# A mixed attention and long-convolution kernel: softmax shift and sum as identity matmuls, fused parameter steps, an input load in eight chained pieces, a new task order

## The chip, the cores and the metric

The kernel runs on one core of one Trainium2 chip, in one launch. The metric is the device time of an execution in microseconds (us), lower is better. Five instruction queues run side by side on the core: TensorE (PE in the profile, its weight loads PEld), VectorE (DVE), ScalarE (ACT), GpSimd (POOL) and SyncE (SP). Each works strictly through its own list of instructions; a semaphore makes an instruction wait for another queue. POOL and SP here mostly issue DMA transfers.

## The reference

`x` and `u` in the kernel are one tensor, `A_x`, 2048 rows of 640 in bf16 (`B_u` is not read). The result is a gated sum of two branches:

```python
# A: sliding-window attention, H=32 heads of 20, window W=8, dilation 2
qkv = x @ wqkv                                    # [2048,640] @ [640,1920]
logits[h,s,w] = (q[h,s] . k[h,s-2w]) * 20**-0.5   # -1e9 where s-2w < 0
a = (softmax_w(logits) weighted sum of v[h,s-2w]) @ wo
# B: state-space convolution, N=192 complex states per channel
dt = exp(log_dt); P = exp(dt*(A_re + 1j*A_im) * l)          # l = 0..2047
K[d,l] = Re sum_n C[d,n] * P[d,n,l] * dt*B[d,n]
y = irfft(rfft(u, 4096) * rfft(K, 4096))[:2048] + u*Dskip
g = sigmoid((x*gate_w).sum(-1))
out = g*a + (1-g)*y
```

## The kernel before

The program has two halves. The first is a set of some 1,200 small tasks. Each names its engine, a duration, what it depends on, the buffers it takes and gives back, and a due time. `Plan.order` (L91) plays these tasks on a model of the queues and always starts the waiting task with the earliest due time; `Plan.emit` (L185) writes the instructions in the order so found. The due times come from the numbers in `PLAN` (L48). So what stands behind what on each queue is fixed before the launch, and a table of numbers sets it. The second half, `fft_conv` (L959), is written out by hand.

The tasks, in the order in which they become possible:

- **Parameters** (`SSMParams.build`, L544). From C, B, A and dt, all [640,192] and held as 128 x 960 in float32, come the phase step (`tau`, `x1`), the log decay (`xa`), the log magnitude (`xl`) and the angle (`at`) of each state. `tt` (L584) is a two-tensor operation on VectorE, `ts` (L588) a tensor with two scalars, `stt` (L591) a fused (tensor op scalar) op tensor, `act` (L594) a ScalarE function. `ratio` (L634) finds min/max of two magnitudes with a VectorE reciprocal (L637); `angle1` to `angle3` (L652 to L669) set the quadrant; `wrap` (L597) takes a phase modulo 65536 by adding and subtracting a large constant. `split` (L613) cuts each result into two or three bf16 pieces (a ScalarE copy `pc`, L607, and a VectorE remainder, L611), and SP stores the twelve pieces to `Sprm` in DRAM.
- **Transposes and projections.** `window` (L224) turns x into `xT` by identity matmuls (L239). `plan_late` (L302) computes q, k and v: 60 tasks of five 128x512 matmuls (L324), each evicted from PSUM by ScalarE or VectorE (L477/L479) and stored by POOL (L339). ScalarE or VectorE is chosen by the planner for every eviction.
- **Attention** (`plan_core`, L343), in eight chunks of 256 rows. POOL loads `qc`, `kc`, `vc` (L364). Five VectorE products `prod` (L373) go through indicator matmuls into the logits bank `lg` in PSUM (L379), one bank for all chunks. `subtract` (L386): a VectorE maximum over the window (L391) and a VectorE subtraction into `lgs` (L393), which frees `lg`. `expo` (L396): exp on ScalarE. `probs` (L398): VectorE sum (L401), reciprocal (L403), multiplication (L405). SP stores the weights and loads them back spread over partitions (`asb`, L408 and L412). Then five VectorE products with v (L429), identity matmuls that sum over the window (L434), the output projection (L451), and the gate (L460/L462).
- **Convolution kernel** (`KGen.plan`, L718), in ten chunks of 16 channels in each of four groups. SP loads `L` from `Sprm` with eight small transfers (L716), into two buffers; TensorE forms the arguments `ar` (L743, L748); ScalarE takes sin (L760) and exp (L762); VectorE multiplies (`pt`, `qq`, L783 to L785); TensorE sums into `kps` (L801). sin and exp lie in different function tables of ScalarE, each change costs an `ACT_TABLE_LOAD`. After chunks 5 and 10 the half is laid out through DRAM (`KExpand`, L819) and back into `kc`.
- **First transform step** (`first`, L1155): `Usb`, which is x in another layout, and the two halves `kc` are multiplied with `F1c` (L1163). `Usb` shares its memory with `xn`, the buffer of projections (`prj`); its load can only start when the last projection is stored. POOL issues it as four transfers of 640 KB (`rows`, L937; tasks at L1174), followed by `omF` (L943).

The second half multiplies spectra (L994 to L1013), transforms back (L1027, L1047), adds the attention branch and stores.

## Time and profile before

| what | value |
|---|---|
| three runs | 395.54, 396.29, 397.03 us (median 396.29) |
| the profiled execution's own time | 394.38 us |
| its span, first to last instruction | 392.6 us |
| mean granted TensorE clock | 0.923 |
| busy: PE / DVE / ACT / POOL | 319.8 / 333.3 / 307.1 / 79.4 us |
| DMA moved | 58.82 MB |

The profile is of one execution, in microseconds from the first instruction. A row of grouped instructions names source line, engine, operation, output<-input and count, then busy time and the mean duration of one, then the idle time of the engine just ahead of them and what ended most of it. The table of stretches gives, for each stretch of the span, the busy time of each engine (and its number of instructions), the granted TensorE clock (1.00 is full), the busy share of the DMA engines and GB/s. In a row of the timeline the two first numbers are start and duration, and a bracket at its end holds the idle time ahead of it. "issue" stands for a wait for which the profile shows no releaser.

### The profile page before, as it was taken

The page shows a single profiled execution, that of the slowest core. Times are in us where ns is not written, and L with a number is a line of the kernel's source. Part 1 is how long each engine was busy: PE and PEld are TensorE (multiplying, and loading weights), DVE is VectorE, ACT ScalarE, POOL GpSimd, SP SyncE. Part 2 cuts the span into 40 slices and gives each one's busy share as a digit, 9 for nine tenths or more (in the row PEclk, how much of TensorE's full clock was granted, in tenths as well). Part 3 has the DMA queues.
Part 4 walks back from the last instruction along what each step waited for, and adds up shares of the span by engine and source line. Part 5 has one row for each costly group of instructions (what it writes and reads, how often), then busy time and mean ns, then how long its engine had stood idle before and what let it go on. Part 6 is the DMA issues. An engine that isn't in the chain of part 4 may idle for free.

```text
span 392.6 us, 11691 instructions
## 1 busy us (share of the span) xinstructions
PE 319.8 (81%) x5026; PEld 189.5 (48%) x5046; DVE 333.3 (85%) x428; ACT 307.1 (78%) x434; POOL 79.4 (20%) x111
## 2 busy tenths in 40 slices
PE   0299899998979879889676889789999889995770
PEld 0266454443534344454324335446777655554770
DVE  5499999888989999998869785999999459999782
ACT  1489876469889999998769677978977599995791
POOL 8932122320310101004520100100110022100044
PEclk9999999999998989899978656959999999999996
DMA  8965569765721343124995640412481069925046
GB/s 275 372 174 162 175 211 270 206 176 198 216 69 46 104 112 117 45 77 156 193 242 169 203 114 16 127 40 77 155 240 46 35 161 243 225 56 215 2 109 161
DMA packets 51463, 58.82 MB, mean 150 GB/s; under 512 B 36180, under 2 KB 43220, under 8 KB 51156
## 3 DMA queue, kind: packets, MB, share of 16 engines
q1 hardware_dynamic: 41492, 28.78, 27.0%
q0 software_dynamic: 8192, 28.69, 25.0%
q8 instruction: 39, 0.64, 0.7%
q10 hardware_dynamic: 1728, 0.61, 0.6%
q14 instruction: 12, 0.10, 0.1%
HBM read 38.29 MB, written 19.77 MB: 148 GB/s over the span
## 4 chain that ended last, share of the span: by engine, by line
PE 45%; DVE 26%; ACT 14%; issue 6%; DMA 5%; POOL 1%; SPq 1%; POOLq 0%; ACTq 0%; DVEq 0%
PE tb L324 8%; PE tb L434 7%; PE tb L451 5%; PE ar L743 5%; PE fp L994 5%; PE kps L801 5%; PE bp L1163 5%; DVE pv L429 3%; DMA xn<-in_A_x_dram 3%; ACT big L762 3%; ACT sp_u L997 3%; DVE bufA L955 3%; PE lg L379 3%; ACT sp_k L997 3%; DVE qq L785 2%
## 5 line engine op out<-in xcount | busy, mean ns | idle before, releaser
L760 ACT ACTIVATE big<-ar 128x608 bf16<-128x608 int16 x96 | 59.8, 676 | 18.0 <-PE ar L743 9.7
L324 PE MATMUL tb<-bufA 128*128 128x512 bf16 x287 | 70.3, 384 | 4.1 <-DVE prj L479 1.1
L762 ACT ACTIVATE big<-ar 128x864 bf16<-128x864 f32 x60 | 49.6, 909 | 1.9 <-PE ar L743 1.4
L373 DVE TENSOR_TENSOR prod<-qc,kc 128x2048 bf16<-128x2048 bf16 x40 | 47.8, 1219 | 2.2 <-PE lg L379 2.2
L324 PEld LDWEIGHTS <-bufA 128*128 128x128 bf16 x300 | 33.5, 119 | 33.0 <-issue 9.1
L429 DVE TENSOR_TENSOR pv<-vc,asb 128x2048 bf16<-128x2048 bf16 x40 | 47.1, 1218 | 2.6 <-PE tb L434 2.6
L743 PE MATMUL ar<-Rarg,L 64*128 64x304 bf16 (+1 forms) x320 | 39.5, 302 | 6.6 <-ACT big L762 2.6
L434 PE MATMUL tb<-pv,ident 128*128 128x512 bf16 (+1 forms) x185 | 39.3, 352 | 0.9 <-issue 0.5
L801 PE MATMUL kps<-qq,pt 128*32 128x22 bf16 (+1 forms) x2560 | 31.1, 176 | 6.4 <-issue 4.5
L801 PEld LDWEIGHTS <-pt 128*32 128x32 bf16 (+1 forms) x2560 | 24.5, 95 | 21.1 <-issue 15.7
L994 PEld LDWEIGHTS <-PHI 128*128 128x128 bf16 x256 | 24.8, 97 | 19.0 <-issue 8.8
L451 PE MATMUL tb<-wo_sb,oT 128*128 128x320 bf16 x160 | 30.8, 332 | 1.2 <-issue 1.1
L748 PE MATMUL ar<-Rarg,L 64*64 64x304 bf16 (+1 forms) x320 | 22.0, 308 | 11.6 <-issue 4.8
L743 PEld LDWEIGHTS <-L 64*128 64x128 bf16 x320 | 13.6, 96 | 29.3 <-issue 26.3
L477 ACT ACTIVATE prj<-tb 128x512 bf16<-128x512 f32 x30 | 17.8, 596 | 10.5 <-PE tb L324 10.3
L434 PEld LDWEIGHTS <-ident 128*128 128x128 bf16 x192 | 18.0, 100 | 15.9 <-issue 3.2
L997 ACT ACTIVATE sp_k<-fp 128x1280 bf16<-128x1280 f32 x16 | 19.1, 1236 | 4.6 <-DVE om L979 3.0
L994 PE MATMUL fp<-big,PHI 128*128 128x320 bf16 x128 | 19.2, 298 | 3.2 <-ACT sp_k L997 3.2
L785 DVE TENSOR_TENSOR qq<-big 128x1408 bf16<-128x1408 bf16 x24 | 21.2, 884 | 0.0
L451 PEld LDWEIGHTS <-oT 128*128 128x128 bf16 x160 | 15.7, 106 | 11.1 <-issue 4.6
L994 PE MATMUL fp<-bufA,PHI 128*128 128x320 bf16 x128 | 19.1, 298 | 2.3 <-ACT sp_u L997 1.5
L997 ACT ACTIVATE sp_u<-fp 128x1280 bf16<-128x1280 f32 x16 | 19.1, 1237 | 1.8 <-PE fp L994 1.8
(188 smaller groups left out, 601.4 us busy)
## 6 DMA issues: line engine op xcount, KB each, us to landing
asb<-aS SPq DMA_DIRECT2D x8, 512.0 KB, 4.1
PSI<-c_psi SPq DMA_DIRECT2D x8, 512.0 KB, 8.0
PHI<-c_phi POOLq DMA_DIRECT2D x8, 384.0 KB, 5.0
Sprm<-pc SPq DMA_DIRECT2D x12, 240.0 KB, 2.3
L<-Sprm SPq DMA_DIRECT2D x80, 36.0 KB, 2.9
kc<-kS POOLq DMA_DIRECT2D x8, 337.5 KB, 4.3
vc<-vS POOLq DMA_DIRECT2D x8, 337.5 KB, 4.8
xn<-in_A_x_dram SPq DMA_DIRECT2D x4, 640.0 KB, 11.7
```

The lines of the kernel that those rows point to most:

```text
L324: nc.tensor.matmul(ppf, self.wq[:, kt, which * D + e:(which + 1) * D:5], self.xT[:, c0 // 1024, kt, c0 % 1024:c0 % 1024 + SC], start=(kt = ...
L373: nc.vector.tensor_tensor(b[e][:], b["qc"][:, e, :].unsqueeze(1).to_broadcast([128, W, C]), win(b["kc"][:, e, :], 0, W, DIL, C), ALU.mult)
L429: nc.vector.tensor_tensor(b["pv", e][:, :, k, :].rearrange("p w (b t) -> p w b t", t=64), for_e, aw, ALU.mult)
L434: nc.tensor.matmul(b["op", e][:, 0:n, :], ident[:], b["pv", e][:, w, 0:n, :], start=(w == 0), stop=(w == W - 1))
L451: nc.tensor.matmul(apf[:, :320], b["oT"][:, e, i * 128:(i + 1) * 128], wo_sb[:, e, hf * 320:(hf + 1) * 320], start=(e == 0), stop=(e == 4))
L743: nc.tensor.matmul(ar[:, g2, a0:a0 + ncol], L[rows, gp, sb, NST * u:NST * u + 128], R[rows, c0:c0 + ncol], start=True, stop=True, tile_pos ...
L760: nc.scalar.activation(dst[:, 2 * gp:2 * gp + 2, sub, :], ar[:].bitcast(I16)[:, :, 0:2 * SW:2], ACT.Sin, scale=SCL)
L762: nc.scalar.activation(dst[:, 2 * gp:2 * gp + 2].rearrange("p g s n -> p g (s n)"), ar[:, :, 0:2 * EW], ACT.Exp)
L785: nc.vector.tensor_tensor(qq[:], trg[:, :, KI:].rearrange("p a (v m) -> p a v m", v=2), exq[:, :, KI:].unsqueeze(2).to_broadcast([128, 32, ...
L801: nc.tensor.matmul(kps[32 * g:32 * g + 32, c2, NM * ql:NM * ql + NM], pt[rows, k, v, :], qq[rows, k, v, :], start=(g not in started), stop ...
L994: nc.tensor.matmul(fp[:, fl, 0:320].rearrange("p (c x) -> p c x", x=32), PHI[:, fl, kind, :], B[:, :, 2 * f1 + ri].rearrange("p c q g -> p ...
L997: nc.scalar.activation(t[:], fp[:, :, 0:320].rearrange("p f (x g) -> p x f g", g=4), ACT.Identity)
```

## The change

Five things change; the second half of the program is the same.

1. **Softmax.** VectorE still takes the maximum. It then writes the negated maximum as two bf16 tiles of 128x64, `hi` and the remainder `lo`. TensorE adds both into the logits bank with two identity matmuls of 512 columns. exp reads the bank itself and writes bf16. TensorE sums over the window with eight identity matmuls of 64 columns, into the first 64 columns of the same bank. VectorE's reciprocal reads them, and the product is made in place. `lgs` is gone, `at` has two buffers, and the bank is given back only after the reciprocal.
2. **Parameters.** The VectorE reciprocal becomes exp(-ln) on ScalarE and one Newton step on VectorE; many pairs of `ts` and `tt` become one `stt`; the constant steps of `wrap` may go to either engine (`lin`).
3. **Input load.** `Usb` comes in eight transfers of 320 KB. Ahead of each but the first, POOL copies two elements of the piece before, and so waits for its landing.
4. **Added constraints.** The `prod`, `pv` and `pq` tasks keep their chunk order, and the arguments of convolution chunk 8 (c = 7) come after the transposition step of the first half.
5. **Order.** New numbers in `PLAN`, an offset for single tasks, and a few earlier or later readiness times.

```diff
-            ql=119.5, vl=-141.7, pw=2.2, el=-59.4, tl=47.4, vw=0.0, gate=375.0, l=[80.6, 3.2, 98.5, 133.8, 84.1, 71.9, 127.7, 125.4, 107.0, 224.4, 76.7, 167.3],
+            txw=191.1, ql=135.4, vl=-242.7, pw=18.0, el=-653.5, tl=53.4, vw=216.1, gate=2445.0,
...
-             "lgs": 2, "at": 1, "asb": 2, "pv": 2, "oT": 1, "ga": 1, "prj": 4, "prjw": 3, "pc": 4}
+             "at": 2, "asb": 2, "pv": 2, "oT": 1, "ga": 1, "prj": 4, "prjw": 3, "pc": 4}
...
-            t.due = round(t.due, 3)
+            t.due = round(t.due + pr.get("off", {}).get(t.idx, 0.0), 3)
...
-                if act.get(w - 1, 0) < 2930 and x > 25 and not pr.get("warm"):
+                if act.get(w - 1, 0) < 2930 and x > 70 and not pr.get("warm"):
...
-                b["lgs"] = wk.tile([128, W, 64], F32, name="lgs")
-                nc.vector.tensor_tensor(b["lgs"][:], lg[:], mx[:].unsqueeze(1).to_broadcast([128, W, 64]), ALU.subtract)
+                b["hi"] = wk.tile([128, 64], BF16, name="hi", bufs=1)
+                b["lo"] = wk.tile([128, 64], BF16, name="lo", bufs=1)
+                nc.vector.tensor_scalar(b["hi"][:], mx[:], -1.0, None, ALU.mult)
+                nc.vector.scalar_tensor_tensor(b["lo"][:], mx[:], -1.0, b["hi"][:], ALU.mult, ALU.subtract)
+
+            def lower(_, b=b):
+                for k in ("hi", "lo"):
+                    nc.tensor.matmul(b["lg"][:], ident[:], b[k][:].unsqueeze(1).to_broadcast([128, W, 64]), start=False, stop=(k == "lo"), skip_group_check=True)
 
             def expo(_, b=b):
-                nc.scalar.activation(b["lgs"][:], b["lgs"][:], ACT.Exp, scale=scale)
+                b["at"] = wk.tile([128, W, 64], BF16, name="at")
+                nc.scalar.activation(b["at"][:], b["lg"][:], ACT.Exp, scale=scale)
+
+            def total(_, b=b):
+                for w in range(W):
+                    nc.tensor.matmul(b["lg"][:, 0, :], ident[:], b["at"][:, w, :], start=(w == 0), stop=(w == W - 1), skip_group_check=True)
 
             def probs(_, b=b):
-                lg = b["lgs"]
-                sm = wk.tile([128, 64], F32, name="sm", bufs=1)
-                nc.vector.tensor_reduce(sm[:], lg[:].rearrange("p w t -> p t w"), AX.X, ALU.add)
                 rs = wk.tile([128, 64], F32, name="rs", bufs=1)
-                nc.vector.reciprocal(rs[:], sm[:])
-                b["at"] = wk.tile([128, W, 64], BF16, name="at", bufs=1)
-                nc.vector.tensor_tensor(b["at"][:], lg[:], rs[:].unsqueeze(1).to_broadcast([128, W, 64]), ALU.mult)
+                nc.vector.reciprocal(rs[:], b["lg"][:, 0, :])
+                nc.vector.tensor_tensor(b["at"][:], b["at"][:], rs[:].unsqueeze(1).to_broadcast([128, W, 64]), ALU.mult)
...
-            ts(tmp, src, float(mul / 65536.0), MAGIC, ALU.mult, ALU.add)
-            ts(tmp, tmp, MAGIC, 65536.0, ALU.subtract, ALU.mult)
+            lin(tmp, src, mul / 65536.0, MAGIC)
+            lin(tmp, tmp, 65536.0, -MAGIC * 65536.0)
...
-            tt("t0", "t0", "ax", "ay", ALU.max)
-            ts("t0", "t0", 1e-30, None, ALU.max, ALU.bypass)
-            op("recip", "D", 6.1, lambda _: V.reciprocal(t0[:], t0[:]), ["t0"], ["t0"])
+            stt("t0", "ax", 1e-30, "ay", ALU.max, ALU.max)
+            op("act_s0", "A", 0.95, lambda _: SCA.activation(t["s0"][:], t["t0"][:], ACT.Ln), ["t0"], ["s0"], table="ln")
+            op("act_s1", "A", 0.95, lambda _: SCA.activation(t["s1"][:], t["s0"][:], ACT.Exp, scale=-1.0), ["s0"], ["s1"], table="exp")
+            tt("s0", "s0", "t0", "s1", ALU.mult)
+            stt("t0", "s0", 2.0, "s1", ALU.subtract, ALU.mult)
...
-            ts("t0", "wr", 0.0, None, ALU.is_lt, ALU.bypass)
-            ts("t1", "at", -2.0, float(np.pi), ALU.mult, ALU.add)
-            tt("t1", "t1", "t1", "t0", ALU.mult)
-            tt("at", "at", "at", "t1", ALU.add)
+            lin("t1", "at", 1.0, float(-np.pi / 2))
+            stt("t1", "wr", 0.0, "t1", ALU.is_lt, ALU.mult)
+            stt("at", "t1", -2.0, "at", ALU.mult, ALU.add)
...
+            g0, h0 = (n - 1) // 2, (n - 1) % 2
+            nc.gpsimd.tensor_copy(P["pace"][32 * g0:32 * g0 + 32, :], P["Usb"][32 * g0:32 * g0 + 32, 32 * h0, 0:2])
+        nc.gpsimd.dma_start(P["Usb"][32 * g:32 * g + 32, 32 * h:32 * h + 32], x.rearrange("(a b) d -> a b d", b=64)[:, 32 * h:32 * h + 32, 160 * g:160 * g + 160])
```

What the new numbers do is seen in the order of the instructions. Rows are those of the built program, without their numbers; equal neighbours are merged (x2), and L is the source line of the version concerned.

**VectorE around the phase step and the reciprocal of the parameters, before** (`t_143` and `t_144` are two scratch tiles, `ax` and `ay` the magnitudes, `aim` the input that comes last):

```order
L586 TENSOR_TENSOR wr<-wr,t_143 128x960
L586 TENSOR_TENSOR wi<-wi,t_144 128x960
L586 TENSOR_TENSOR tau<-aim,dtb 128x960
L589 TENSOR_SCALAR s_154<-tau 128x960
L479 CAST bufA<-ar 128x1024
L589 TENSOR_SCALAR s_154<-s_154 128x960
L592 SCALAR_TENSOR_TENSOR tau<-tau,s_154 128x960
L586 TENSOR_TENSOR t_143<-ax,ay 128x960
L589 TENSOR_SCALAR t_143<-t_143 128x960
L637 RECIPROCAL t_143<-t_143 128x960
L611 TENSOR_TENSOR s_154<-tau,pc 128x960
```

**and now:**

```order
L604 TENSOR_TENSOR wr<-wr,t_144 128x960
L604 TENSOR_TENSOR wi<-wi,t_145 128x960
L654 TENSOR_TENSOR dt_139<-dtb 128x5
L610 SCALAR_TENSOR_TENSOR t_144<-ax,ay 128x960
L604 TENSOR_TENSOR t_145<-ax,ay 128x960
L604 TENSOR_TENSOR tau<-aim,dtb 128x960
L604 TENSOR_TENSOR xl<-xl,xa 128x960
L604 TENSOR_TENSOR xl<-xl,dt_139 128x960
L610 SCALAR_TENSOR_TENSOR tau<-tau,s_155 128x960
L492 CAST bufA<-ar 128x1024
L637 TENSOR_TENSOR s_155<-tau,pc 128x960
```

Maximum and minimum of the magnitudes stand ahead of the step that reads `aim`, the two constant steps of the wrap have left VectorE at this place, and the reciprocal is gone.

**VectorE at the softmax of the second attention chunk, before** (`prj<-tb` evicts a projection, `pv` is a product with v of the chunk ahead):

```order
L391 TENSOR_REDUCE mx<-lg 128x64
L393 TENSOR_TENSOR lgs<-lg,mx 128x512
L479 CAST prj<-tb 128x512 x3
L401 TENSOR_REDUCE sm<-lgs 128x64
L403 RECIPROCAL rs<-sm 128x64
L405 TENSOR_TENSOR at<-lgs,rs 128x512
L479 CAST prj<-tb 128x512
L429 TENSOR_TENSOR pv<-vc,asb 128x8x256 x4
```

**and now:**

```order
L395 TENSOR_REDUCE mx<-lg 128x64
L398 TENSOR_SCALAR hi<-mx 128x64
L399 SCALAR_TENSOR_TENSOR lo<-mx,hi 128x64
L442 TENSOR_TENSOR pv<-vc,asb 128x8x256 x2
L492 CAST prj<-tb 128x512 x2
L415 RECIPROCAL rs<-lg 128x64
L416 TENSOR_TENSOR at<-at,rs 128x512
L377 TENSOR_TENSOR prod<-qc,kc 128x2048 x5
```

Two products with v and two evictions stand between maximum and reciprocal, where three evictions stood; the products of the next chunk come behind the reciprocal.

**POOL around the load of `Usb`, before** (`qS` is the store of a projection, `qc`, `kc`, `vc` are loads for attention, `Kx` the layout of the first convolution half):

```order
L364 DMA vc<-vS 128x5x270
L364 DMA kc<-kS 128x5x270
L339 DMA qS<-prj 640x1x512
L940 DMA Usb<-in_A_x_dram 32x64x160 x4
L943 DMA omF<-omS 32x128 x2
L364 DMA qc<-qS 128x5x256
L364 DMA vc<-vS 128x5x270
L943 DMA omF<-omS 32x128 x2
```

**and now:**

```order
L343 DMA vS<-prj 640x1x512
L343 DMA qS<-prj 640x1x512
L970 DMA Usb<-in_A_x_dram 32x32x160
L969 COPY pace<-Usb 32x2
L970 DMA Usb<-in_A_x_dram 32x32x160
L368 DMA qc<-qS 128x5x256
L368 DMA kc<-kS 128x5x270
L368 DMA vc<-vS 128x5x270 x2
L969 COPY pace<-Usb 32x2
L970 DMA Usb<-in_A_x_dram 32x32x160
L969 COPY pace<-Usb 32x2
L970 DMA Usb<-in_A_x_dram 32x32x160
```

One piece at a time is under way, and the attention loads stand between the pieces; the first piece follows the last two stores of projections directly.

More of the change, by code (lines that the diff above doesn't have):

```diff
@@ L412, in spread @@
                 nc.sync.dma_start(b["asb"][:].rearrange("p b x -> p (b x)"), self.aS[sc % 2].rearrange("h b x -> h (b x)").unsqueeze(1).to_broadcast([32, 4, W * C]))
[L413 to L416 removed]
+            mx = pl.add(f"max{sc}", "D", 0.90, top, deps=[l], due=due(5 * pr["pw"]))
+            ng = pl.add(f"neg{sc}", "P", 0.45, lower, deps=[mx], due=due(5 * pr["pw"]), eq=1024)
+            ex = pl.add(f"exp{sc}", "A", 0.55, expo, deps=[ng], acq=["at"], due=due(5 * pr["pw"] + pr["el"]), table="exp")
+            sm = pl.add(f"sum{sc}", "P", 0.40, total, deps=[ex], due=due(5 * pr["pw"] + pr["el"]), eq=512)
+            at = pl.add(f"at{sc}", "D", 1.17, probs, deps=[sm], rel=[("lg", lgs[0])], due=due(5 * pr["pw"] + pr["el"] + pr["tl"]))
+            st = pl.add(f"ast{sc}", "S", 0.4, store, deps=[at], rel=[("at", ex)], due=due(0.0), dma=0.45)
             asb = pl.add(f"asb{sc}", "S", 0.55, spread, deps=[st], acq=["asb"], due=due(0.0), dma=1.6)
@@ L577, in build @@
         tau, x1, xa, xl_, at, s0, s1 = (f(n) for n in ("tau", "x1", "xa", "xl", "at", "s0", "s1"))
+        bias = {}
+        for c in (MAGIC, -MAGIC * 65536.0, 1e-36, float(-np.pi / 2)):
+            bc = pin.tile([128, 1], F32, name=f"bc{len(bias)}")
+            nc.vector.memset(bc[:], c)
+            bias[c] = bc[:]
         ops = []
@@ L671, in build @@
         for step in [weights, phase, squares, st[0], ratio, size, st[1], st[2], lambda: wrap("x1", "tau", 256.0, "t0"), sl[0], sl[1], angle1, sx[0],
[L672 removed]
+                     sx[1], angle2, sx[2], lambda: tt("xa", "xa", "are", "dtb", ALU.mult, rdy=21.0), sa[0], angle3, sa[1], sp[0], sp[1]]:
             step()
@@ L806, in plan @@
                 due = d0 + dd * (0.55 + 0.16 * u) + pr["dl"][c]
-                p = pl.add(f"pq{c}{u}", "D", 2.04, products, deps=ends[u, 0] + ends[u, 1], acq=["pq"], rel=[("trg", held[u, 0]), ("exq", held[u, 1])], due=due)
+                p = pl.add(f"pq{c}{u}", "D", 2.04, products, deps=ends[u, 0] + ends[u, 1], after=self.pqs[-1:], acq=["pq"], rel=[("trg", held[u, 0]), ("exq", held[u, 1])], due=due)
                 self.pqs.append(p)
```

79 lines of the change are left out of this document (43 added, 36 removed), and 3 rows, old and new, of the table f0.

## The prediction

> **What bounds the kernel now.** I read the span first, then the table of stretches, then the rows in the stretch where all engines fall off together. The stretches are cut where the work changes: from 17 us the input is there, 59 ends most of the parameters, 100 to 265 is convolution kernel and attention together, from 309.6 the second half runs.
>
> ```profile
> span 392.6 us, 11691 instructions
> ...
> 17.00:59.00 42.00, 38.80 (x287) 23.57 (x292) 40.25 (x40) 35.68 (x47) 12.26 (x19) 1.00 0.63 193
> 59.00:100.00 41.00, 39.22 (x228) 17.83 (x232) 36.51 (x46) 28.49 (x43) 11.07 (x14) 1.00 0.71 210
> 100.00:185.00 85.00, 73.45 (x1879) 38.73 (x1883) 81.28 (x111) 77.72 (x117) 9.32 (x11) 0.94 0.34 102
> 185.00:200.00 15.00, 9.99 (x266) 5.04 (x262) 10.12 (x13) 9.04 (x16) 7.39 (x10) 0.84 1.04 192
> 200.00:265.00 65.00, 54.74 (x1109) 27.96 (x1107) 55.35 (x71) 53.53 (x77) 5.58 (x9) 0.70 0.43 127
> 265.00:309.60 44.60, 44.03 (x564) 32.81 (x567) 39.91 (x56) 36.85 (x50) 3.19 (x5) 1.00 0.37 114
> 309.60:392.60 83.00, 58.84 (x709) 43.11 (x707) 61.47 (x88) 61.32 (x85) 14.78 (x24) 0.96 0.59 143
> ```
>
> The columns behind the length are PE, PEld, DVE, ACT and POOL busy, the granted clock, the DMA share and GB/s. VectorE is busy for 40.25 of 42 us while the parameters are made and for 81.28 of 85 us in the middle; TensorE has 39.22 of 41 from 59 to 100 and 44.03 of 44.6 from 265. So VectorE limits two stretches, TensorE two. From 185 to 200 nothing is full but the DMA engines (1.04), and from 200 to 265 the clock is 0.70 and VectorE down to 55.35 of 65. The rows of the hole:
>
> ```profile
> 183.40 4.20 POOL L940 DMA_DIRECT2D Usb<-in_A_x_dram  x4 [4.00 <-PE ar L743]
> 184.47 6.13 SPq L716 DMA_DIRECT2D L<-Sprm  x8
> 198.22 0.46 PE L748 MATMUL ar<-Rarg,L 64*64 64x304 bf16 x1 [4.82 <-issue]
> 198.78 0.68 ACT L760 ACTIVATE big<-ar 128x608 bf16<-128x608 int16 x1 [4.62 <-PE ar L748]
> 199.71 0.69 DVE L391 TENSOR_REDUCE mx<-lg 128x64 f32<-128x512 f32 x1 [4.88 <-PE lg L379]
> ...
> DMA to landing us min/median/max: 2.9/11.0/15.3
> ```
>
> The last line is of the `L` loads from 170 to 202 us. POOL issues the four parts of `Usb` at once; the eight small `L` transfers that SP issues a microsecond later need up to 15.3 us instead of 2.9. The argument matmul of the next chunk reads `L`; it stands for 4.82 us, and ScalarE (4.62) and VectorE (4.88) behind it.
>
> **The change part by part.** The sum is made against the profiled execution's own 394.4 us (span 392.6 and 1.8 around it); the median of the three runs, 396.3, lies 1.9 higher, and the predicted time is for the median.
>
> *Parameters.* Durations:
>
> ```profile
> L637 DVE RECIPROCAL t<-t 128x960 f32<-128x960 f32 x1 | 6.2, 6152 | 0.0
> L589 DVE TENSOR_SCALAR t<-t 128x960 f32<-128x960 f32 x4 | 2.8, 710 | 0.1
> L586 DVE TENSOR_TENSOR t<-t,t 128x960 f32<-128x960 f32 x3 | 3.5, 1152 | 0.0
> L592 DVE SCALAR_TENSOR_TENSOR tau<-tau,s 128x960 f32<-128x960 f32 x1 | 1.2, 1159 | 0.0
> ...
> L607 ACT ACTIVATE pc<-s 128x960 bf16<-128x960 f32 x7 | 7.0, 1000 | 0.5 <-DVE s L611 0.3
> L595 ACT ACT_TABLE_LOAD x2 | 2.6, 1283 | 0.0
> ...
> 15.27 1.16 DVE L586 TENSOR_TENSOR tau<-aim,dtb 128x960 f32<-128x960 bf16 x1 [3.73 <-DMA aim<-in_B_A_im_dram]
> ```
>
> By the order, VectorE loses the reciprocal (6.15), 7 of 13 two-scalar operations (7 x 0.71 = 5.0) and 6 of 26 two-tensor ones (6 x 1.15 = 6.9), and gains 9 fused ones (9 x 1.16 = 10.4): 7.6 us less. ScalarE gains four operations of 1.0 and one table load of 1.28 here (five stand in this part instead of four, 17 instead of 18 in the program): 5.3 us beside VectorE, covered as long as ScalarE keeps up; it has 35.68 of 42 us now, so what it gains must partly be taken from it, and the order does that (below). Maximum and minimum now stand in the 3.73 us in which VectorE waits for `aim`: up to 2 us more. That pays for a new wait in the first softmax, where only one eviction stands between maximum and reciprocal (some 2 us by the chain worked out under the third rival); I count both as nothing.
>
> *Softmax.* Durations, the last row but one being the smallest VectorE operation with two scalars:
>
> ```profile
> L391 DVE TENSOR_REDUCE mx<-lg 128x64 f32<-128x512 f32 x8 | 5.5, 688 | 6.8 <-PE lg L379 6.6
> L393 DVE TENSOR_TENSOR lgs<-lg,mx 128x512 f32<-128x512 f32 x8 | 5.5, 692 | 0.3
> L401 DVE TENSOR_REDUCE sm<-lgs 128x64 f32<-128x512 f32 x8 | 8.3, 1032 | 0.9 <-ACT lgs L396 0.8
> L403 DVE RECIPROCAL rs<-sm 128x64 f32<-128x64 f32 x8 | 4.4, 553 | 0.3
> L405 DVE TENSOR_TENSOR at<-lgs,rs 128x512 bf16<-128x512 f32 x8 | 5.5, 692 | 0.3
> ...
> L266 DVE TENSOR_SCALAR omg<-g_sb 128x16 f32<-128x16 f32 x1 | 0.2, 174 | 0.0
> ...
> L396 ACT ACTIVATE lgs<-lgs 128x512 f32<-128x512 f32 x8 | 5.1, 631 | 0.0
> ```
>
> Subtraction (0.69) and sum (1.03) go in each of eight chunks: 13.8 us. Maximum, reciprocal and product stay, and I leave their prices. `hi` and `lo` are new, 16 operations on 64 columns, between 0.17 (16 columns) and 0.55 (the 64-column reciprocal, which is slow for its size): 2.8 to 8.8 us. I take 0.2 each, near the plain operation, 3.2 us. VectorE saves 10.6, with ends of 5.0 and 11.0. exp stays one instruction of about 0.63.
>
> TensorE's added work is bounded by these rows:
>
> ```profile
> 176.93 1.90 PE L434 MATMUL tb<-pv,ident 128*128 128x512 bf16 x8
> ...
> L255 PE MATMUL ar<-gw_sb,bufA 128*128 128x1 bf16 x80 | 2.1, 163 | 0.0
> L239 PE MATMUL ar<-ident,xn 128*128 128x128 bf16 x80 | 7.7, 256 | 14.2 <-DMA xn<-in_A_x_dram 13.7 <-ACT bufA L477 0.3
> ```
>
> Sixteen matmuls of 512 columns at 1.90/8 = 0.24 are 3.8 us. The 64 of 64 columns lie between 2.1/80 = 0.026 (1 column) and 7.7/80 = 0.096 (128): 1.7 to 6.1 us, taken in the middle at 0.06, 3.8. Together 7.6.
>
> *Evictions.* The new order gives ten evictions from ScalarE to VectorE.
>
> ```profile
> L479 DVE CAST prj<-tb 128x512 bf16<-128x512 f32 x15 | 10.2, 684 | 2.3 <-PE tb L324 2.1
> L479 DVE CAST big<-bp 128x1024 bf16<-128x1024 f32 x3 | 3.7, 1220 | 0.5 <-PE bp L1163 0.5
> L477 ACT ACTIVATE prj<-tb 128x512 bf16<-128x512 f32 x30 | 17.8, 596 | 10.5 <-PE tb L324 10.3
> ```
>
> Four have 512 columns (4 x 0.68), two net have 1024 (2 x 1.22), four are narrower (0.68 at most, taken at 0.45): 6.9 us onto VectorE. ScalarE loses about the same, which pays for its 5.3.
>
> VectorE's net is -7.6 - 10.6 + 6.9 = -11.3 us. Its work from 17 to 265 stands now at 40.25 + 36.51 + 81.28 + 10.12 + 55.35 = 223.5 in 248 us.
>
> *Input load.* The prices and the first reader:
>
> ```profile
> kc<-kS POOLq DMA_DIRECT2D x8, 337.5 KB, 4.3
> ...
> L940 POOL DMA_DIRECT2D Usb<-in_A_x_dram x4 | 4.2, 1058 | 4.0 <-PE ar L743 4.0
> L975 POOL COPY PSI<-sp_u 128x2 bf16<-128x2 bf16 x4 | 3.4, 841 | 2.1 <-ACT sp_u L997 2.1
> ...
> L1163 PEld LDWEIGHTS <-Usb x80: 158/161/163, 274.8 to 309.2; 128*128 128x128 bf16 x80
> ```
>
> With one piece under way, an `L` load meets 320 KB instead of 2.6 MB; a transfer of that size lands in 4.3 us, so the 4.9 us hole (VectorE's 4.88) goes. A piece costs POOL at most an issue of 1.06, a landing of 4.3 and a copy of 0.84, 6.2 us, eight of them 50. Even if the chain starts at 183.4 as now, it ends near 233, ahead of the first reader at 274.8 (some 259 after the gain); by the order it starts earlier, since the last projection stores stand earlier. Behind each waiting copy stand attention loads (`qc`, `kc`, `vc`) and behind the last the store of `Kx`; a load can come up to 6.2 us late. I price that at nothing, because those loads are issued ahead of their products.
>
> The added order constraints and the 83.0 us of the second half cost nothing: same instructions, same order.
>
> **Sum:** -11.3 (VectorE) - 4.9 (hole) = -16.2; 394.4 - 16.2 = 378.2 for an execution like the profiled one, 380 for the median.
>
> What is late next is TensorE. It has 38.80 + 39.22 + 73.45 + 9.99 + 54.74 = 216.2 us of work from 17 to 265, and 223.8 with 7.6 more, in a stretch of 232. That is 96%; the best the trace shows before 265 is 78.0 of 83 us, 94%. The sum therefore needs part of the slow clock of 200 to 265 back. I expect that, because the hole stands right ahead of the fall from 0.94 to 0.70.
>
> [...]
>
> **The rivals.**
>
> *TensorE becomes the bound.* The clock stays at 0.70 where it is 0.70, because between 200 and 265 no wait of TensorE is long:
>
> ```profile
> PE kps L801 <- issue: 2.0, 2, 1.4
> ```
>
> This is the longest there, 1.4 us, so the low clock can have a cause other than the hole, and the change adds two waits of TensorE per chunk (for `lo`, for exp). Then 223.8 us at 94% need 238 us: -10, 384.4, 386 for the median, and 389 with the dearer small matmuls. Against it: the clock was 0.94 to 1.00 until the hole. Chance 0.24. [...]
>
> *The clock comes back fully.* From 200 to 265 VectorE works at the share of 100 to 185 (81.28/85 = 0.956 instead of 55.35/65 = 0.852): 65 x 0.104 = 6.8 us more, -23, 373 for the median. For it: every stretch without the hole ahead of it is at 0.94 or better. Against: it asks for 98% of TensorE unless the faster clock shortens its work. Chance 0.15.
>
> *Slower: the softmax becomes a chain through three in-order queues, on one bank.* Between maximum and product now lie `hi`/`lo`, two matmuls, exp, eight matmuls and the reciprocal. One hand-over costs what VectorE loses at a product:
>
> ```profile
> 70.22 1.23 DVE L373 TENSOR_TENSOR prod<-qc,kc 128x2048 bf16<-128x2048 bf16 x1 [0.31 <-PE lg L379]
> ```
>
> Four of 0.31, with 0.4 + 0.48 + 0.63 + 0.5, are 3.2 us, 4.5 with a table load. If TensorE reaches the sum before exp is done, the arguments and `kps` matmuls behind it wait, and ScalarE and VectorE after them; and no next logits can start while the bank is held. It decides from 16.2/8 = 2 us lost per chunk. At 3 us, 24 in all, the time is 402, 404 for the median. Against it: in all chunks but the first, four to eleven operations stand between `lo` and the reciprocal on VectorE, 3 us and more. Chance 0.10.
>
> That the change does nothing, because the work it takes off VectorE lay under TensorE's time everywhere, would need -4.9 to be lost as well: 0.03.
>
> **How the numbers follow.** The forecast has 0.48, 380. The range runs from 368 (the second rival with the cheaper end of the unknown prices, and a little of the clock for TensorE) to 392 (the first rival with `hi` and `lo` at the dear end); it leaves out the slower case and tails, about 0.15. A measurement of this kernel tells about 0.5% (2 us; the three runs lie 1.5 apart) from no change. Faster: 0.48 + 0.24 + 0.15, less the upper tail of the first rival, 0.85. Slower 0.10, same 0.05.
>
> **What would show it.** Right: VectorE's work from 17 us to the second half down by about 11; the `L` loads landing within 6 us and no idle above 2 us on PE, ACT and DVE at once; a second half of 83 us. The first rival shows as PE above 94% busy with a clock near 0.7; the third as idle time on VectorE ahead of the reciprocal (L415) and on TensorE ahead of its sum (L411) of 2 us per chunk. The parameter term is wrong if VectorE waits for ScalarE before 55 us, the load term if VectorE waits for products of a late `vc` or TensorE for `Usb`.

## The result and the profile after

| | before | after |
|---|---|---|
| median of four runs each | 396.66 us (395.54 to 397.70) | 384.59 us (384.40 to 385.24) |
| profiled execution, its span | 394.38, 392.6 us | 384.76, 383.0 us |
| first matmul of the second half | 311.0 us | 302.0 us |

The ratio is 0.9732, with an interval of 0.9686 to 0.9778: faster, by 12.1 us in the medians and by 8.8 to 12.5 us by the ratio's interval on 396.7 us. The forecast was 380 (368 to 392), a gain of 16. The gain of the profiled executions, 9.6 us, lies in the first half (9.0). Here and below, the ratios leave out executions over 1.5% above the fastest of their kernel (two of them, of 1,493 and 710 us, far above), while medians are of all.

The profile after, first the span and the busy times, then the same stretches as before (PE, PEld, DVE, ACT, POOL busy, clock, DMA share, GB/s; the second half now begins at 302):

```profile
span 383.0 us, 11863 instructions
...
PE 316.9 (83%) x5102; PEld 191.0 (50%) x5126; DVE 323.0 (84%) x437; ACT 304.1 (79%) x427; POOL 89.3 (23%) x122
```

```profile
17.00:59.00 42.00, 35.07 (x266) 21.27 (x271) 38.55 (x40) 37.54 (x47) 12.86 (x20) 0.96 0.72 212
59.00:100.00 41.00, 39.34 (x279) 17.76 (x279) 30.38 (x44) 28.38 (x43) 8.80 (x11) 1.00 0.54 160
100.00:185.00 85.00, 77.40 (x1720) 41.42 (x1731) 79.02 (x105) 74.33 (x113) 16.79 (x23) 1.00 0.52 144
185.00:200.00 15.00, 14.10 (x471) 7.82 (x470) 14.65 (x30) 12.66 (x20) 10.41 (x7) 0.93 0.47 117
200.00:265.00 65.00, 55.77 (x1330) 30.54 (x1331) 59.09 (x84) 55.66 (x78) 7.31 (x13) 0.83 0.42 121
...
300.00:383.00 83.00, 60.52 (x714) 44.96 (x712) 62.23 (x88) 61.74 (x85) 14.71 (x24) 0.93 0.63 143
```

VectorE's work fell by 333.3 - 323.0 = 10.3 us (forecast 11.3); from 17 us to the second half it fell by 12.4, since some of it moved ahead of 17. The stretch from 185 to 200 has lost its hole: TensorE has 14.10 us of work in it instead of 9.99. The clock from 200 to 265 rose from 0.70 to 0.83, not to 1. From 59 to 100 TensorE is as full as before and VectorE now idles 10.6 us: there its saving became waiting.

The prices of the new softmax, by groups (busy, mean ns, idle time ahead):

```profile
L407 ACT ACTIVATE at<-lg 128x512 bf16<-128x512 f32 x8 | 4.8, 605 | 0.0
...
L415 DVE RECIPROCAL rs<-lg 128x64 f32<-128x64 f32 x8 | 4.4, 553 | 2.1 <-PE lg L411 1.9
...
L403 PE MATMUL lg<-hi,ident 128*128 128x512 bf16 x8 | 3.3, 413 | 0.0
...
L411 PE MATMUL lg<-at,ident 128*128 128x64 bf16 x64 | 3.2, 193 | 0.2
...
L398 DVE TENSOR_SCALAR hi<-mx 128x64 bf16<-128x64 f32 x8 | 2.1, 257 | 0.3
...
L399 DVE SCALAR_TENSOR_TENSOR lo<-mx,hi 128x64 bf16<-128x64 f32 x8 | 1.8, 225 | 0.3
```

`hi` and `lo` cost 0.24 each (taken at 0.2), the 64 small matmuls 3.2 us (taken at 3.8). The 413 ns of a matmul on `hi` is its own length; the one on `lo` starts 0.22 to 0.26 us behind it in seven chunks of eight, near the 0.24 taken. Ahead of the reciprocal VectorE waits 2.1 us in all eight chunks together.

The timeline of TensorE just ahead of the hole of before; then that of the kernel after where it stops now; then, after, the time of the `L` loads from issue to landing:

```profile
192.96 0.45 PE L748 MATMUL ar<-Rarg,L 64*64 64x304 bf16 x7
```

```profile
212.62 0.64 PE L826 MATMUL kps<-qq,pt 64*32 64x22 bf16 x63
215.88 0.41 PE L826 MATMUL kps<-qq,pt 64*32 64x22 bf16 x33 [2.61 <-issue]
```

```profile
DMA to landing us min/median/max: 1.7/2.6/5.1
```

Before, the seven matmuls are a whole task of four and three of the next, all of one chunk. The fourth of that next task, which reads the same `L`, came only at 198.22; TensorE had stopped at 193.4 us. The earlier tasks of the chunk (L743, up to 191.6 us) had read every part of this `L`, so no wait for `L` can stand there. The prediction had the wrong cause. After, `L` lands in 5.1 us at most, and TensorE again stops in the middle of a task, for 2.61 us.

What both stops have in common is in the DMA table. Its row of the instruction queue, after:

```profile
q8 instruction: 40, 0.66, 0.7%
```

Forty packets, each of 16,384 bytes in the trace; TensorE's list has 5,126 matmuls and as many weight loads, so a packet would hold some 256 of its instructions, or 128 pairs (an estimate: 2 x 5,126 / 40). The times of these packets, taken from the trace, against the end of each wait of TensorE for "issue" (us):

```
kernel   wait of TensorE   it goes on at   packet lasted        goes on after its end by
before        4.82            198.22       195.32 to 196.77          1.45
before        1.44            230.25       227.84 to 228.93          1.32
before        1.14            111.88       109.20 to 110.27          1.61
after         2.61            215.88       213.61 to 214.57          1.31
after         0.79            137.50       135.01 to 135.90          1.60
```

In thirteen profiles of this case (before, after and the eleven kernels of the table below) TensorE has 67 waits of over 0.4 us for "issue". Every one of them ends 1.20 to 1.61 us after such a packet has ended. Every one also stands at the same place of TensorE's list: counted in weight loads from its start, 92 or 93 past a multiple of 128, whatever the instruction there is. That is the estimated size of a packet, and I read it so: TensorE had run out of instructions, and the packet with the next ones was late. This rests on these times and counts; no run shows the instructions themselves arriving. Below, waits for instructions are waits of this kind. In the first row of the table the packet started only 1.9 us after TensorE had stopped. (A first profile of the kernel before with the pieces, the execution of 1,493 us, is not among the thirteen: it has 20 such waits, of 0.74 to 0.94 us, none of which ends 1.2 to 1.6 us after a packet, and their cause is open.)

### The profile page after: what moved, and what is told of

Its sections match the earlier page's. It is cut to its first block, busy times and chain, and to the rows that moved or that the text cites. A ratio compares the mean times of both kernels' runs of the same rounds, so it can differ in the third digit from the quotient of the medians.

```text
span 383.0 us, 11863 instructions
## 1 busy us (share of the span) xinstructions
PE 316.9 (83%) x5102; PEld 191.0 (50%) x5126; DVE 323.0 (84%) x437; ACT 304.1 (79%) x427; POOL 89.3 (23%) x122
## 4 chain that ended last, share of the span: by engine, by line
PE 51%; ACT 19%; DVE 13%; DMA 9%; issue 5%; SPq 1%; POOL 1%; POOLq 0%; ACTq 0%; DVEq 0%
PE tb L328 13%; PE tb L447 7%; PE ar L768 6%; PE fp L1024 5%; PE tb L464 5%; PE kps L826 4%; PE bp L1195 3%; DMA aim<-in_B_A_im_dram 3%; ACT big L787 3%; ACT sp_u L1027 3%; ACT big L785 3%; PE lg L383 3%; DVE bufA L985 3%; ACT sp_k L1027 3%; PE ar L773 2%
## 5 line engine op out<-in xcount | busy, mean ns | idle before, releaser
L328 PE MATMUL tb<-bufA 128*128 128x512 bf16 x283 | 71.5, 388 | 6.5 <-DVE bufA L492 2.1
L785 ACT ACTIVATE big<-ar 128x608 bf16<-128x608 int16 x96 | 59.6, 677 | 10.2 <-PE ar L768 9.4
L768 PE MATMUL ar<-Rarg,L 64*128 64x304 bf16 (+1 forms) x320 | 37.0, 290 | 5.8 <-ACT big L785 2.4
L826 PE MATMUL kps<-qq,pt 128*32 128x22 bf16 (+1 forms) x2560 | 30.2, 175 | 4.6 <-issue 4.2
L826 PEld LDWEIGHTS <-pt 128*32 128x32 bf16 (+1 forms) x2560 | 23.3, 93 | 17.5 <-issue 12.3
L464 PE MATMUL tb<-wo_sb,oT 128*128 128x320 bf16 x160 | 27.7, 310 | 0.0
L490 ACT ACTIVATE prj<-tb 128x512 bf16<-128x512 f32 x28 | 16.5, 598 | 10.9 <-PE tb L328 9.9
L959 POOL DMA_DIRECT2D PHI<-c_phi x8 | 4.5, 558 | 79.5 <-PE fp L1024 41.7
L773 PE MATMUL ar<-Rarg,L 64*64 64x304 bf16 (+1 forms) x320 | 19.6, 298 | 3.8 <-ACT big L787 1.6
L243 PE MATMUL ar<-ident,xn 128*128 128x128 bf16 x80 | 7.9, 263 | 15.6 <-DMA xn<-in_A_x_dram 14.1
## 6 DMA issues: line engine op xcount, KB each, us to landing
PSI<-c_psi SPq DMA_DIRECT2D x8, 512.0 KB, 10.2
xn<-in_A_x_dram SPq DMA_DIRECT2D x4, 640.0 KB, 12.4
```

The source lines that it names most:

```text
L328: nc.tensor.matmul(ppf, self.wq[:, kt, which * D + e:(which + 1) * D:5], self.xT[:, c0 // 1024, kt, c0 % 1024:c0 % 1024 + SC], start=(kt = ...
L464: nc.tensor.matmul(apf[:, :320], b["oT"][:, e, i * 128:(i + 1) * 128], wo_sb[:, e, hf * 320:(hf + 1) * 320], start=(e == 0), stop=(e == 4))
L768: nc.tensor.matmul(ar[:, g2, a0:a0 + ncol], L[rows, gp, sb, NST * u:NST * u + 128], R[rows, c0:c0 + ncol], start=True, stop=True, tile_pos ...
L773: nc.tensor.matmul(ar[64 * h:64 * h + 64, g2, a0:a0 + ncol], L[rows, h, sb, m0:m0 + 64], R[rows, c0:c0 + ncol], start=True, stop=True, til ...
L785: nc.scalar.activation(dst[:, 2 * gp:2 * gp + 2, sub, :], ar[:].bitcast(I16)[:, :, 0:2 * SW:2], ACT.Sin, scale=SCL)
L826: nc.tensor.matmul(kps[32 * g:32 * g + 32, c2, NM * ql:NM * ql + NM], pt[rows, k, v, :], qq[rows, k, v, :], start=(g not in started), stop ...
```

## The experiments

Theory A is the prediction's: VectorE sets the pace of the first half, what is taken from it is passed on, TensorE's new work lies beside it, and the pieces take the late `L` loads away. Theory B: TensorE has become the bound. On the load the rival is the late instruction packet. All times are of several timed runs beside the kernel before; ratios are to it, and "on the kernel after" is the difference of the ratios times 396.7 us. By both intervals, taken as independent, such a difference is uncertain by 2.2 to 2.7 us, by 3.3 for the four dense matmuls alone and by 3.6 for `Kx` spread.

| kernel | median us | ratio (interval) | on the kernel after |
|---|---|---|---|
| after, old softmax | 395.57 | 0.9986 (0.9948 to 1.0023) | +10.1 |
| after, more matmuls | 395.13 | 0.9990 (0.9958 to 1.0022) | +10.2 |
| after, old reciprocal | 389.46 | 0.9831 (0.9782 to 0.9880) | +3.9 |
| after, `Usb` at once | 396.42 | 1.0034 (1.0000 to 1.0067) | +12.0 |
| before, with pieces | 392.54 | 0.9926 (0.9887 to 0.9965) | (-2.9 on before) |
| after, old softmax and reciprocal | 398.35 | 1.0038 (0.9992 to 1.0084) | +12.1 |
| after, `Kx` spread | 382.48 | 0.9646 (0.9567 to 0.9726) | -3.4 |
| after, four dense matmuls | 387.52 | 0.9829 (0.9759 to 0.9899) | +3.8 |
| `Kx` spread, useless burst | 384.35 | 0.9721 (0.9679 to 0.9762) | -0.4 |
| `Kx` spread, no `lo` | 381.02 | 0.9610 (0.9559 to 0.9661) | -4.8 |
| the last, four dense matmuls | 381.83 | 0.9628 (0.9578 to 0.9678) | -4.1 |

**Old softmax in the new order.**

```diff
-                nc.vector.tensor_scalar(b["hi"][:], mx[:], -1.0, None, ALU.mult)
-                nc.vector.scalar_tensor_tensor(b["lo"][:], ...)
+                nc.vector.tensor_tensor(b["lgs"][:], lg[:], mx[:]..., ALU.subtract)
...
-                nc.tensor.matmul(b["lg"][:], ident[:], b[k][:]..., ...)
...
-                    nc.tensor.matmul(b["lg"][:, 0, :], ident[:], b["at"][:, w, :], ...)
+                nc.vector.tensor_reduce(sm[:], b["lgs"][:]..., AX.X, ALU.add)
```

> The kernel after with the old softmax put back in its place, all tasks in the new order: VectorE subtracts the maximum and sums over the window (8 x (0.69 + 1.03) = 13.8 us) instead of writing hi and lo (2.1 + 1.8 = 3.9 us), TensorE gives up the two shift matmuls and the eight sums of every chunk (3.3 + 3.3 + 3.2 = 9.8 us by their rows, some 7 by throughput). Theory A, VectorE sets the pace of the first half and its work is passed on one for one: +9.9 us on the kernel after. Theory B, TensorE sets the pace since the change: VectorE's 9.9 us hide and TensorE's 7 to 9.8 us come off, so -7 to 0. Between the two (+2 to +7): the engines are so evenly loaded that work moved between them counts in part.

+10.1 us: theory A's number. VectorE's 9.9 us were worth their full time, although the matmuls went away with them. The number is not VectorE's alone: in this profile TensorE waits 8.3 us for instructions up to the second half (waits over 0.4 us; 4.8 after), and 11 windows of slow clock stand there where the kernel after has 8.

**More matmuls.**

```diff
             def total(_, b=b):
+                for _k in range(4):
+                    nc.tensor.matmul(b["lg"][:], ident[:], b["at"][:], start=True, stop=True, skip_group_check=True)
```

> The kernel after with four more identity matmuls of 512 columns ahead of every window sum, whose result the sum overwrites: 32 x 0.24 = 7.7 us more on TensorE, nothing on VectorE or ScalarE. Theory A (VectorE sets the pace): within 1 us of the kernel after. Theory B (TensorE sets the pace): +7 us or more. A third reading is that more activity keeps TensorE's clock up, which would make it faster.

+10.2 us for 7.7 us of work: theory B's side. Added work on TensorE is not free. In the profile TensorE is busy 15.2 us longer (332.1 against 316.9), and two of the extra slow windows come late, from 255 and 371 us. Its waits for instructions sum to 7.9 us instead of 4.8; with the 7.7 that makes 10.8, so a late packet may be what made the work dearer than its price. So neither theory holds alone: from this balance, work added to either engine is paid. Why taking TensorE's work away in the run before gave nothing back stays open; the waits named there are a candidate.

**Old reciprocal.**

```diff
-            stt("t0", "s0", 2.0, "s1", ALU.subtract, ALU.mult)
+            op("stt_t0", "D", 1.1, lambda _: V.reciprocal(t["t0"][:], t["t0"][:]), ["s0", "s1"], ["t0"])
```

with the logarithm, the exponential and the product ahead of it left out.

> The kernel after with the parameter reciprocal back on VectorE in the place of the last Newton operation, everything else in the new order: VectorE gains 6.15 and loses 1.16 + 1.16, +3.8 us; ScalarE loses two operations of 1.0 and a table load of 1.28. Theory A (VectorE sets the pace): +3.8 us on the kernel after. Theory B (the parameters lie under TensorE's work): 0. If ScalarE is what the parameters wait for: -2.

+3.9 us, theory A. In the profile the first maximum of the softmax stands 3.6 us later (74.3 against 70.7): passed on from the start. The close agreement of the total is partly luck, since its uncertainty is 2.7 us and the waits for instructions differ too (8.0 us in this profile, the longest of the six executions, against 4.8).

**`Usb` at once.**

```diff
-            nc.gpsimd.tensor_copy(P["pace"][...], P["Usb"][...])
-        nc.gpsimd.dma_start(P["Usb"][32 * g:32 * g + 32, 32 * h:32 * h + 32], ...)
+        for g in range(4):
+            nc.gpsimd.dma_start(P["Usb"][32 * g:32 * g + 32], ...)
```

> The kernel after with Usb loaded as four transfers of 640 KB at once, at the place of the first piece, without the waiting copies; the order of all engines but POOL stays. The prediction's theory, late L loads: L lands some 10 us late, TensorE's first argument matmul of a convolution chunk waits for a DMA, +4.9 us on the kernel after. Rival, the instruction fetch: TensorE stands 3 to 5 us in the middle of a task, with no releaser in the profile, and goes on 1.3 to 1.6 us after a 16 KB packet of the instruction queue has ended; no wait for L stands ahead of it. If the burst at this place does not fall on a stretch in which TensorE takes short instructions, both give 0, and the attention loads, no longer behind waits for landing, come earlier: -1.

+12.0 us, and neither number: the burst starts at 152.9 us, and what it hits there is a third thing. VectorE, then TensorE, in that run:

```profile
163.39 0.42 DVE L492 CAST oT<-tb 128x256 bf16<-128x256 f32 x1 [0.69 <-PE tb L447]
172.89 1.01 DVE L475 TENSOR_SCALAR ga<-tb,g_sb 128x320 bf16<-128x320 f32 x2 [9.08 <-DMA gaS<-ga]
...
177.41 4.63 DVE L442 TENSOR_TENSOR pv<-vc,asb 128x2048 bf16<-128x2048 bf16 x4 [2.32 <-DMA vc<-vS]
```

```profile
173.50 1.49 PE L464 MATMUL tb<-wo_sb,oT 128*128 128x320 bf16 x5 [7.73 <-DVE ga L475]
```

VectorE waits 9.08 us for the store of the chunk ahead, which was issued at 158.26 and has the buffer `ga`, then 2.32 for `vc`. The loads of `vc` issued from 152 to 172 us landed in 17.5 us, against 4.9 in the kernel after. Here the burst delayed the transfer that was needed next; which one that is depends on the order. Both explanations of the load term were too narrow.

**Pieces alone, in the kernel before.** The rows are those of the kernel after; POOL issues the first piece where the four transfers stood and the others between the attention loads behind.

```diff
-        nc.gpsimd.dma_start(P["Usb"][32 * g:32 * g + 32], ...)
+            nc.gpsimd.tensor_copy(P["pace"][...], P["Usb"][...])
+        nc.gpsimd.dma_start(P["Usb"][32 * g:32 * g + 32, 32 * h:32 * h + 32], ...)
```

> The kernel before, all engines in its own order; only POOL loads Usb in eight chained pieces, the first where the four transfers stood, the others between the attention loads behind. Both theories on the hole (late L loads, late instruction fetch) expect the 4.8 us wait of TensorE at 193 us to go: -4.9 us on the kernel before. If the slow clock from 195 to 263 us came from the hole, it goes too: -10 to -12 in all. If the pieces are worth nothing by themselves, 0, and the gain of the kernel after is that of its other parts.

> A second profile of the kernel before with the pieces alone, 392.54 us in the timed runs, since the first profiled execution was disturbed. Late instruction fetch: no wait of TensorE over 2 us near 193 us, and smaller ones that each end 1.2 to 1.6 us after an instruction packet; the slow windows from 195 on fewer than 13, by two or three only, since a gain of 3 us leaves no room for more. If the 4.8 us wait is still there, the pieces gained elsewhere.

-2.9 us (1.4 to 4.5) where 4.9 were forecast. The second profile, 389.54 us, shows the place on the timeline (L752 is L748 of before), and the `L` loads from 170 to 202 us:

```profile
193.51 0.45 PE L752 MATMUL ar<-Rarg,L 64*64 64x304 bf16 x7
195.83 0.31 PE L752 MATMUL ar<-Rarg,L 64*64 64x304 bf16 x1 [1.88 <-issue]
```

```profile
DMA to landing us min/median/max: 1.8/4.7/5.0
```

The wait is down from 4.82 to 1.88 us, between the same two matmuls, with `L` landing in 5.0 us at most; it ends 1.20 us after a packet of the instruction queue. Of 13 slow clock windows from 195 us to the second half 9 are left, and 14 of 16 from the start.

**Old softmax and old reciprocal together** (both edits above).

> The kernel after with both the old softmax and the old reciprocal, in the new order: what is left of the change are the order, the pieces, the other parameter steps and the constraints. If the two costs add up as measured one by one (+10.0 and +3.9 on the kernel after): 398 to 399, no better than the kernel before. If they hide each other in part: 393 to 396. If VectorE had not been what limits: 385 to 388.

398.35 us, ratio 1.0038: the two costs add up nearly (12.1 against 14.0). So order, pieces, evictions and the other parameter steps together are worth +1.5 us (-0.3 to +3.3) against the kernel before, where the prediction's terms for them make -3.75 - 4.9 + 6.9 = -1.75.

**`Kx` spread.** At 208 us the kernel after sends 1.3 MB of `Kx` at once, from SP and POOL.

```diff
+            if hf == 0:
+                if e == "S":
+                    return
+                for n in (0, 2):
+                    nc.gpsimd.dma_start(Kx[n:n + 2]..., x[:, n:n + 2, 0:8]...)
+                    nc.gpsimd.tensor_copy(x[:, n, 0, 0:2], x[:, n, 0, 0:2])
+                nc.gpsimd.dma_start(Kx[4:8]...[1], x[1::2, 4:8, 1:9]...)
+                nc.gpsimd.tensor_copy(x[:, 4, 8, 0:2], x[:, 4, 8, 0:2])
```

> The kernel after with the three stores of Kx for the first convolution half (1.28 MB at once at 208 us) sent by POOL as four of 320 KB, each behind the landing of the one before, and the four loads of kc behind them, on POOL too. Theory, bursts hold up the instruction fetch: the 2.6 us wait of TensorE at 213 us goes, and with it the idle window that starts the six slow clock windows from 215 to 235 us; -2.6 from the wait alone, up to -10 with the clock. Rival, the slow windows come from the small matmuls there and not from the wait: -1 to -3. Cost: kc lands near 240 us instead of 223, ahead of its first matmul at 246; if it is later than that, TensorE waits for it and the gain is lost.

-3.4 us in the timed runs, not clear of the 3.6 us of uncertainty, and between the numbers of theory and rival (a profiled execution of 377.3 us span against 383.0). Stretches after, then with `Kx` spread, columns as above:

```profile
210.00:220.00 10.00, 6.79 (x231) 3.35 (x231) 7.25 (x10) 6.82 (x10) 1.68 (x3) 0.75 0.81 271
220.00:230.00 10.00, 9.57 (x254) 4.55 (x257) 9.93 (x15) 9.35 (x15) 0.00 (x0) 0.50 0.57 158
230.00:240.00 10.00, 9.50 (x193) 4.36 (x195) 9.65 (x12) 8.72 (x13) 0.32 (x1) 0.73 0.01 3
```

```profile
210.00:220.00 10.00, 8.36 (x295) 4.88 (x293) 10.00 (x14) 9.88 (x17) 4.33 (x4) 1.00 0.49 166
220.00:230.00 10.00, 9.03 (x195) 4.02 (x197) 9.93 (x14) 8.87 (x14) 7.05 (x7) 0.66 0.29 82
230.00:240.00 10.00, 8.88 (x345) 5.43 (x340) 9.97 (x14) 9.12 (x12) 1.70 (x3) 1.00 0.83 233
```

The wait at 213 us is gone, VectorE is full through the whole 30 us, and of six slow windows two are left. The first matmul on `kc` comes at 240.2 us without a wait. That the burst of `Kx` goes with the hole is seen in the other profiles too: in all seven kernels in the new order that send it at once (after, old softmax, more matmuls, old reciprocal, `Usb` at once, both old parts, four dense matmuls) a wait of TensorE for instructions of 2.3 to 3.9 us ends 5 to 9 us behind its first store. In the three that spread it and have no burst in its place, there is none there (twice) or one of 1.2 us.

**A useless burst.** Only SP's list gets one row more:

```diff
+                    nc.sync.dma_start(self.junk[:], self.x[0:960, 0:512])
```

> The spread-Kx kernel with one transfer more, which nobody reads: SP copies 983 KB of x into a spare DRAM tensor at 208 us, as many bytes as the two Kx stores had there that it no longer issues. No engine waits for it. Theory, a burst holds up the instruction fetch: TensorE's wait of 2 to 4 us near 213 us, which ends 1.2 to 1.6 us after a packet of the instruction queue, comes back, and with it most of the six slow clock windows: +3 to +6 us on the spread-Kx kernel. Rival, the gain of that kernel came from its other order of loads and stores: 0. If the kc loads land after 240 us, TensorE waits for them, and the reading is spoilt by that much.

+3.0 us on the `Kx` spread kernel, at the low end of what was expected; the intervals overlap by 0.5%, so the time alone does not settle it. In the profile the wait is back, smaller:

```profile
210.91 0.66 PE L826 MATMUL kps<-qq,pt 64*32 64x22 bf16 x63
213.00 0.38 PE L826 MATMUL kps<-qq,pt 64*32 64x22 bf16 x33 [1.43 <-issue]
```

At the place where the kernel after had 2.61 us stand 1.43 us, 1.40 after an instruction packet's end, and six slow windows begin at 213.6 us. But the kernel without `lo` (below), which spreads `Kx` and has no useless burst, shows nearly the same in its profile, 1.42 us after a packet:

```profile
211.28 0.69 PE L826 MATMUL kps<-qq,pt 64*32 64x22 bf16 x69
213.16 0.34 PE L826 MATMUL kps<-qq,pt 64*32 64x22 bf16 x27 [1.19 <-issue]
```

There too six slow windows follow, from 213.8 us. So a wait of this size and the slow stretch can come without the burst, and this run does not show that bytes which no engine waits for hold up TensorE. The evidence that a burst does this stays that of `Usb` and `Kx` above.

**Four dense matmuls.**

```diff
+                        for _k in range(4 if sc == 6 else 0):
+                            nc.tensor.matmul(b["lg"][:]..., ident[:], b[e][:, 0:2, :]..., start=True, stop=True, skip_group_check=True)
```

> The kernel after with four dense matmuls (128 x 128 by 512 columns) ahead of the first logits of the seventh attention chunk, at 217 us, whose result the logits overwrite: 1.0 us of TensorE at full clock, 1.9 at half. Theory, the clock follows the array work in each 3.41 us window: the window from 215 us, at 2,066 full-array columns, rises above some 2,800, and the clock is back at 218.4 instead of 235.4 us: five slow windows fewer, -3 to -7 us. Rival, the clock does not follow the work there: +1 to +2 us.

+3.8 us, little more than its uncertainty. It did not test its theory. The first logits of that chunk stand at 210.7 us in the trace, not at 217, so the matmuls filled a window that had enough (3,943 columns from 210.8 us). Then TensorE waits 2.60 and 2.26 us for instructions, and the six slow windows come as in the kernel after.

**No `lo`, with `Kx` spread; then the four matmuls on top.**

```diff
-                nc.vector.scalar_tensor_tensor(b["lo"][:], mx[:], -1.0, b["hi"][:], ALU.mult, ALU.subtract)
...
-                for k in ("hi", "lo"):
+                nc.tensor.matmul(b["lg"][:], ident[:], b["hi"][:]..., start=False, stop=True, skip_group_check=True)
```

> The spread-Kx kernel without lo: the shift is the bf16 rounding of the negated maximum alone, which a softmax allows, since any shift gives the same weights. VectorE loses 8 x 0.225 = 1.8 us, TensorE eight matmuls of 512 columns, 8 x 0.24 = 1.9 (3.3 by their row). If VectorE's work is passed on one for one: -1.8 on the spread-Kx kernel; if TensorE's counts too, as the run with more matmuls says: -3 to -4. If less array work lets the clock fall in more windows: 0 to +3.

> The kernel without lo and with Kx spread, and with the four dense matmuls ahead of the first logits of the seventh chunk. In the spread-Kx kernel the windows from 215.1 and 218.5 us hold 2,447 and 2,469 full-array columns, and the two behind 221.9 are slow; 2,048 more put one of them above 2,800. Theory, the clock follows the array work: the slow windows near 222 go, -2 to -3 us on the kernel without lo after 1.0 us of work is paid. Rival: +1.

381.02 and 381.83 us: both beat the kernel after (0.9610, up to 0.9661, against 0.9686 at least), and neither can be told from the `Kx` spread kernel (-1.4 and -0.7 us, inside the intervals). The matmuls again fell too early (some 4,500 columns in the window from 208.7 us), and two slow windows stand from 222 us as in the `Kx` spread kernel. The timed runs of the kernel without `lo` lie between 377.86 and 386.84 us; its profile, 380.2 us of span, has six slow windows and the one with the matmuls on top, 377.4, two. The six come behind the wait of 1.19 us shown above, which the other profile has not. So single executions of these kernels may differ by whether that packet is late and the slow stretch comes.

## Why the prediction was right, and where not

The time fell inside the range and the mechanism carried: VectorE's work went down by about what was counted, and it was passed on. Four of the sixteen microseconds did not come, and no run shows in full where they went.

- **Softmax, -10.6.** Measured 10.1 by undoing it, with TensorE's share of the change undone too. Right, operation prices included.
- **Parameters, -7.6.** Of this the reciprocal was tested alone: 3.9 for 3.8, with 2.7 of uncertainty. VectorE waits 2.4 us for ScalarE in this part (1.4 for the exponential, 1.0 for `ay`), so the sign that was to show this term wrong is there, but small.
- **Evictions, +6.9.** Not tested alone. By the two profiles three of the ten have 512 columns and five are narrower, not four and four, which changes the term by 0.2. VectorE's busy time, 10.3 less for 11.3 forecast, holds all three terms and agrees.
- **Input load, -4.9: the step that failed.** "With one piece under way, an `L` load meets 320 KB instead of 2.6 MB ... so the 4.9 us hole goes." The loads do land early (5.1 us at most after), but the hole was TensorE without instructions, as far as the packet that ended 1.45 us ahead of its end tells. In the order of before the pieces are worth 2.9, and a wait of 1.88 stays. In the new order a second burst, 1.3 MB of `Kx` with the last piece of `Usb` 5 us ahead, makes a new hole of 2.61 us. The sign that the prediction named, no idle over 2 us on three engines at once, comes out against it: ScalarE waits 2.60 and VectorE 2.41 us behind that hole. The spread of `Kx` takes this hole away and brings the time to 382.5, nearer to the 380 of the sum, but its 3.4 us are not clear of noise. So this hole is the likely place of part of what is missing, but that is not shown.
- **"Part of the slow clock back."** Right as far as it went: 16 slow windows up to the second half became 8, where the full return (the second rival) leaves next to none. (That rival's "98% of TensorE" is 223.8 of 225 us by its own sum, 99%.)
- **The attention loads "priced at nothing", the `Usb` chain ahead of its reader.** Right: POOL waits 22.0 us for landings, VectorE waits 0.5 us for a `vc` in all, the last piece is issued at 202.8 us and first read at 268. Left in one burst, in this order, the load costs 12.0 us, more than the term: the price of a burst is that of its place.
- **TensorE's 7.6 beside VectorE's work.** Too cheap: another 7.7 us cost 10.2. The first rival, TensorE as the bound, still fell in its form: TensorE is 221.7 of 248 us busy from 17 to 265, 89% and not over 94%, and VectorE just as long, 221.7; the clock is 0.83 from 200 to 265. (The 94% was no upper end: TensorE's 39.22 of 41 us from 59 to 100 in the prediction's own table are 96%.) That its 386 us lie nearer to the result than 380 is no support for it, since the kernel with one store spread is at 382.5 with the same matmuls.
- **The slower rival.** VectorE waits 2.1 us ahead of the reciprocal in all, not 2 per chunk; 1.7 of them are in the first chunk, where the prediction had some 2.

The additive check: the old softmax and the old reciprocal put back one by one cost 14.0 us, together 12.1, and what is left of the change is then +1.5 us against the kernel before. The gain of this change is the work taken off VectorE, as far as these runs tell. Pieces, new order, evictions and the rest come out at about nothing together; of these, only the pieces were tested alone in the new order (12.0).

## What to carry to other kernels

A wait with no releaser in the middle of a task was here a hint at the instruction supply: TensorE's 67 waits of over 0.4 us for "issue" all ended 1.20 to 1.61 us after a 16 KB packet of the instruction queue. So set the ends of these packets beside such a wait before looking for a late operand, and count the engine's instructions up to it. Transfers whose data are needed late were better sent in chained pieces (for `Usb` 2.9 us in the order of before, 12.0 in the new one): here a burst of 2.6 MB went with VectorE's wait of 9.08 us for a store, and bursts of 2.6 and 1.3 MB went with TensorE's waits of 4.82 and 2.61 us, by the reading above for its code. For stores the profiles say so, the times not clearly. Price a burst by what stands behind it in that order, not by what it hit in the last one.
